# Building x * v of the next batch inside the last transform step of the current one

## The chip, the cores and the metric

The kernel runs on one core of a Trainium2 chip. The metric is the device time of one execution in microseconds (us), the median of several runs. A ratio is the mean time of one kernel's fast runs over the mean of the other's fast runs of the same rounds, so it isn't quite the ratio of the medians.

Names: PE is the matmul engine (PEld its weight loads), DVE the vector engine, ACT the scalar engine, POOL the GpSimd engine, SP the engine that issues the DMAs.

## The reference

Two blocks follow each other. The first is a long causal convolution over 12,480 positions for 4 batches of 128 channels, the second an MLP over the 49,920 rows of its result.

```python
# x, v: (4, 12480, 128); w_in: (128, 2048); w_out: (2048, 128), all float32
u = x * v
y = irfft(rfft(u, n=2*S) * rfft(h_filt, n=2*S))[:, :S]   # along the sequence
z = (x * y).reshape(B * S, D)
h = z @ w_in
out = (h * np.cos(h)) @ w_out
```

## The kernel before

The convolution is done by matmuls in five stages for each batch: x\*v ("u"), first transform ("f1"), second transform with the product by the filter ("f2"), first inverse ("i1"), last inverse with the product by x ("i2"). All stages work in one large SBUF tile, `slots`. The MLP (called MoE here, as in the code) runs over tiles of 480 rows, in 16 steps a tile. Batch 0 is convolved alone; the convolutions of batches 1 to 3 run between the MoE steps of the rows that are ready.

One MoE step:

```python
ph = ps_h.tile(...)                                   # 4 PSUM buffers
nc.tensor.matmul(ph, w_in_sb[:, c * P:(c + 1) * P], ats[n], ...)
nc.scalar.activation(a, ph, AF.Identity, bias=quarter, scale=INV_TWO_PI)
nc.vector.tensor_scalar(out=k, in0=a, scalar1=ROUND, scalar2=ROUND, ...)  # DVE
nc.gpsimd.tensor_tensor(f, a, k, op=ALU.subtract)                         # POOL
nc.scalar.activation(cs, f, AF.Sin, scale=TWO_PI)     # one step later
nc.vector.tensor_tensor(gt, ph, cs, op=ALU.mult)      # DVE, frees ph
nc.tensor.matmul(acc, w_out_sb[:, c, :], gt, ...)     # four steps later
```

The u stage, a group of 4 rows at a time, two of them mirrored about the middle (cut):

```python
def after(j, _):
    for half in range(2):
        engine.tensor_tensor(xt[:, half, :], xt[:, half, :], vt[:, half, :], op=ALU.mult)
        yield
    # both sums of the mirrored halves, written into slots
    for place, op, e in ((a, ALU.add, nc.gpsimd), (ODD + a, ALU.subtract, nc.vector)):
        e.tensor_tensor(u[0:R, :, place:place + UA, :]..., below, above, op=op)
    yield
```

The order of a convolution, with the share of it that each MoE step carries (cut):

```python
def conv_units(bank, b):
    yield from u_units(b, 4, slots[0:R, :, :, :], nc.vector)
    for i, steps in enumerate(f1_units(bank, slots[0:R, :, :, :])): ...
    yield from f2_units(bank, f2_product)
    for i, steps in enumerate(i1_units(bank)): ...
    yield from i2_units(bank, b)      # tm and xs: 3 buffers, asked for 2 groups ahead

U_STEPS, F1_STEPS, F2_STEPS, I1_STEPS, I2_STEPS = 2.75, 0.8, 2.9, 0.8, 1.6
```

The `*_STEPS` say how many MoE steps one unit of a stage is to lie beside. `tm` is a table of 312 KB a group that i2 multiplies with; it comes from DRAM each time.

## Time and profile before

The kernel took 4146.25 us in the median of the 3 runs known before the change (4143.87 to 4154.5). The profile's lines for its stages, and how to read them, are in the prediction below. What a stage costs **beyond** its MoE steps, at the 1.66 us that a step takes alone, is the measure used throughout: it adds up over the whole program, whereas busy shares don't.

The account further down counts a step where its first activation begins; the prediction counts another instruction (k), and the two differ by one here and there. So the stages u, f1, f2, i1 and i2 of batch 1 stand at 36.9, 45.2, 48.4, 56.0 and 53.8 us here, and f1, f2 and i1 at 43.5, 50.2 and 54.4 in the prediction. Batches 2 and 3 are the same within 4 us a stage.

### The profile page before, as it was taken

To read this page: it belongs to the slowest core of one execution; us is meant where nothing else is said; L and a number is where in the kernel's file an instruction comes from. 1 tells how busy PE (TensorE), PEld (TensorE's weight loads), DVE (VectorE), ACT (ScalarE), POOL (GpSimd) and SP (SyncE) were. 2 spreads that over 40 slices of the span, in tenths; PEclk is the share of its full clock that TensorE was granted. 3 is DMA by queue.
4 is the path that set the end of the run, shared out by engine and by line. 5 is a ranking of instruction groups with operands and counts; after the bars stand their busy time and mean duration, and the time that the engine had idled before them with its cause. 6 is when DMAs were issued, how large, how long until landed. Compare 5 with 4: busy or idle time off the path is not lost.

```text
span 4148.7 us, 49336 instructions
## 1 busy us (share of the span) xinstructions
PE 3885.9 (94%) x13882; PEld 2254.5 (54%) x13882; DVE 3050.5 (74%) x6420; ACT 2534.8 (61%) x4692; POOL 2614.4 (63%) x2441
## 2 busy tenths in 40 slices
PE   5958788899999998999999999999999999999999
PEld 3836583465556653555556644655566544444444
DVE  8657678997888569878876599778765566666666
ACT  1344055686667555666665466766664677777777
POOL 2521556777886457558864477488744577777776
PEclk7567799999999999999999999999999999999999
DMA  3253433212221443112211532022105300000000
GB/s 88 80 162 114 127 109 102 71 53 70 80 71 49 138 143 87 31 40 78 80 30 54 181 95 64 26 66 80 57 15 149 92 20 20 19 20 15 19 20 15
DMA packets 271766, 293.66 MB, mean 71 GB/s; under 512 B 16741, under 2 KB 204101, under 8 KB 271237
## 3 DMA queue, kind: packets, MB, share of 16 engines
q1 hardware_dynamic: 271493, 290.50, 24.0%
q8 instruction: 112, 1.84, 0.2%
q14 instruction: 161, 1.32, 0.1%
HBM read 210.12 MB, written 80.31 MB: 70 GB/s over the span
## 4 chain that ended last, share of the span: by engine, by line
PE 70%; POOL 10%; DVE 7%; DMA 5%; ACT 4%; issue 3%; SPq 0%; POOLq 0%; DVEq 0%; ACTq 0%
PE ph L598 25%; PE acc L622 20%; POOL f L607 7%; PE cv L622 5%; PE cv L415 4%; PE cv L396 4%; PE ps L350 3%; PE cv L365 2%; PE cv L350 2%; ACT cs L612 2%; DMA w<-wd 2%; DVE k L604 2%; PE ph L116 2%; POOL slots L344 1%; DMA hd<-h 1%
## 5 line engine op out<-in xcount | busy, mean ns | idle before, releaser
L607 POOL TENSOR_TENSOR f<-a,k 128x480 f32<-128x480 f32 x1664 | 2003.2, 1204 | 1096.1 <-DVE k L604 1075.1
L598 PE MATMUL ph<-at,w_in_sb 128*128 128x480 f32 x3328 | 1639.9, 574 | 43.7 <-DVE gt L614 41.9
L601 ACT ACTIVATE a<-ph,quarter 128x480 f32<-128x480 f32 x1664 | 1095.2, 658 | 665.1 <-PE ph L598 620.5
L622 PE MATMUL acc<-gt,w_out_sb 128*128 128x480 f32 x2784 | 1364.7, 572 | 16.7 <-ACT ot L627 16.2
L614 DVE TENSOR_TENSOR gt<-ph,cs 128x480 f32<-128x480 f32 x1664 | 1092.0, 656 | 310.9 <-ACT cs L612 283.2
L612 ACT ACTIVATE cs<-f 128x480 f32<-128x480 f32 x1664 | 999.2, 600 | 506.4 <-POOL f L607 504.2
L604 DVE TENSOR_SCALAR k<-a 128x480 f32<-128x480 f32 x1664 | 783.5, 471 | 569.4 <-ACT a L601 553.5
L622 PEld LDWEIGHTS acc<-gt,w_out_sb 128*128 128x128 f32 x2784 | 527.8, 191 | 631.3 <-issue 577.1
L598 PEld LDWEIGHTS ph<-at,w_in_sb 128*128 128x128 f32 x3328 | 592.5, 191 | 450.2 <-issue 271.7
L378 POOL TENSOR_TENSOR slots<-slots,t 120x256 f32<-120x256 f32 x384 | 306.0, 803 | 139.0 <-DVE t L377 132.9
L622 PE MATMUL cv<-gt,w_out_sb 128*128 128x480 f32 x544 | 263.2, 566 | 0.5 <-DVE gt L614 0.5
L365 PE MATMUL ps<-slots,w 124*120 124x256 f32 x384 | 164.5, 572 | 84.3 <-DVE w L250 48.7
L396 PEld LDWEIGHTS cv<-cs,slots 120*96 120x96 f32 x1536 | 178.2, 168 | 70.9 <-issue 58.4
L415 PEld LDWEIGHTS cv<-slots,tm 96*104 96x104 f32 x1440 | 175.4, 168 | 62.4 <-issue 51.5
L396 PE MATMUL cv<-cs,slots 120*96 120x120 f32 x1536 | 185.8, 267 | 7.2 <-POOL slots L378 7.2
L338 DVE TENSOR_TENSOR xt<-xt,vt 104x256 f32<-104x256 f32 x180 | 189.7, 1064 | 0.0
L415 PE MATMUL cv<-slots,tm 96*104 96x128 f32 x1440 | 183.5, 272 | 5.3 <-DMA tm<-td 5.3
L365 PE MATMUL cv<-slots,w 124*120 124x256 f32 x576 | 173.7, 382 | 7.0 <-DMA w<-wd 6.1
L365 PEld LDWEIGHTS ps<-slots,w 124*120 124x120 f32 x384 | 92.6, 267 | 156.2 <-issue 67.7
L350 PEld LDWEIGHTS cv<-c,slots 104*124 104x124 f32 x768 | 133.5, 194 | 66.3 <-issue 53.6
L365 PEld LDWEIGHTS cv<-slots,w 124*120 124x120 f32 x576 | 103.4, 184 | 117.6 <-issue 104.4
L622 PEld LDWEIGHTS cv<-gt,w_out_sb 128*128 128x128 f32 x544 | 103.2, 190 | 116.7 <-issue 114.5
(115 smaller groups left out, 3082.3 us busy)
## 6 DMA issues: line engine op xcount, KB each, us to landing
h<-hd SPq DMA_DIRECT2D x192, 240.0 KB
tm<-td SPq DMA_DIRECT2D x90, 312.0 KB
xt<-in_x_dram SPq DMA_DIRECT2D x120, 208.0 KB
vt<-in_v_dram SPq DMA_DIRECT2D x120, 208.0 KB
xs<-in_x_dram SPq DMA_DIRECT2D x120, 208.0 KB
zd<-zs SPq DMA_DIRECT2D x120, 208.0 KB
zb<-zd SPq DMA_DIRECT2D x104, 240.0 KB
out_dram<-ob SPq DMA_DIRECT2D x104, 240.0 KB
```

Source lines behind the costliest of these rows:

```text
L350: nc.tensor.matmul(ps[0:KE, i * 2 * N1:(i + 1) * 2 * N1], u[:, b, 0:KE, i], c1[0:u.shape[0], :, :].rearrange("p r k -> p (r k)"), start=Tr ...
L365: nc.tensor.matmul(ps[0:N2, i * 2 * D:(i + 1) * 2 * D], w[:, i, :], parts[0:KE, :, k1 + i, :, :], start=True, stop=True)
L378: nc.gpsimd.tensor_tensor(y[:, r], y[:, r], t[:, r], op=op)
L396: nc.tensor.matmul(ps[0:N1, (i * 2 + r) * N2:(i * 2 + r + 1) * N2], parts[0:N2, r, :, b, i], cs[:, r:r + 2, :].rearrange("p c a -> p (c a) ...
L415: nc.tensor.matmul(ps[0:R, i * D:(i + 1) * D], t[:, i, r, :], slots[0:N1, :, place, :], start=(r == 0), stop=(r == 1))
L598: nc.tensor.matmul(ph[:, 0:TOK], w_in_sb[:, c * P:(c + 1) * P], ats[n][:, :], start=True, stop=True)
L601: nc.scalar.activation(a[:, :], ph[:, 0:TOK], AF.Identity, bias=quarter[:, 0:1], scale=INV_TWO_PI)
L604: nc.vector.tensor_scalar(out=k[:, :], in0=a[:, :], scalar1=ROUND, scalar2=ROUND, op0=ALU.add, op1=ALU.subtract)
L607: nc.gpsimd.tensor_tensor(f[:, :], a[:, :], k[:, :], op=ALU.subtract)
L612: nc.scalar.activation(cs[:, :], f[:, :], AF.Sin, scale=TWO_PI)
L614: nc.vector.tensor_tensor(gt[:, :], ph[:, 0:TOK], cs[:, :], op=ALU.mult)
L622: nc.tensor.matmul(accs[n][:, 0:TOK], w_out_sb[:, c, :], gt[:, :], start=(c == 0), stop=(c == NFC - 1))
```

## The change

Its intent is to put the DVE work of u beside the PE work of i2. While i2 of batch b reads `slots`, u of batch b+1 writes into the places just read. For that, i2 must go through mirrored pairs of rows as u does, so each group stores z in two pieces. i2 is stretched to 3.4 MoE steps a group where it holds u. To make room in SBUF, `tm` and `xs` get two buffers there instead of three. Batch 1's u stays a stage of its own, and the whole of batch 1 is squeezed into 368 MoE steps, because its convolution has to be ready in time and now includes u of batch 2.

The core of the diff (cut: the helper for the mirrored order, the split store of z, and the same reordering in the table builder):

```diff
-    U_STEPS, F1_STEPS, F2_STEPS, I1_STEPS, I2_STEPS = 2.75, 0.8, 2.9, 0.8, 1.6
+    U_STEPS, F1_STEPS, F2_STEPS, I1_STEPS, I2_STEPS = 2.2, 0.9, 3.1, 0.9, 1.6
+    I2U_STEPS = 3.4
...
+    def n2s(g):
+        a = g * UA
+        return [*range(H - UA - a, H - a), *range(H + a, H + UA + a)]
...
     def conv_units(bank, b):
-        yield from u_units(b, 4, slots[0:R, :, :, :], nc.vector)
...
-        yield from i2_units(bank, b)
+        if b + 1 == B:
+            yield from i2_units(bank, b, 3)
+            return
+        new = u_units(b + 1, 3, slots[0:R, :, :, :], nc.vector, side="right")
+        for i, steps in enumerate(i2_units(bank, b, 2)):
+            if i >= 4:
+                for _ in range(1 + i % 2):
+                    next(new, None)
+            yield steps * I2U_STEPS / I2_STEPS
+        for steps in new:
+            yield steps
...
+            here = NT * NFC - 3 * NFC
+            less = here / (CONV_STEPS + H // UA * U_STEPS)
+            for steps in u_units(1, 4, slots[0:R, :, :, :], nc.vector):
+                yield steps * less
```

More of the change, by code (lines that the diff above doesn't have):

```diff
@@ L318, in filter_out, with load_group @@
                             below, above, op=op)
+    def n2s(g):
+        a = g * UA
+        return [*range(H - UA - a, H - a), *range(H + a, H + UA + a)]
+    def load_group(t, src, b, a):
+        first = src[b, H - UA - a:H - a, :]
+        nc.sync.dma_start(t[:, :, :], bass.AP(
+            tensor=first.tensor, offset=first.offset,
+            ap=[[N2 * D, R], [(UA + 2 * a) * D, 2], [1, UA * D]]))
     def clear_gap(u):
@@ L328, in u_load @@
             t = pool.tile([R, 2, UA * D], F32, name=name, bufs=n)
-            first = src[b, H - UA - a:H - a, :]
-            nc.sync.dma_start(t[:, :, :], bass.AP(
-                tensor=first.tensor, offset=first.offset,
-                ap=[[N2 * D, R], [(UA + 2 * a) * D, 2], [1, UA * D]]))
+            load_group(t, src, b, a)
             tiles.append(t)
@@ L411, in i2_mm @@
         for i in range(part * G // 2, (part + 1) * G // 2):
-            n2 = g * G + i
+            n2 = n2s(g)[i]
             places = (n2 - H, 2 * H + n2) if n2 >= H else (N2 - 1 - n2, N2 + H - 1 - n2)
@@ L416, in i2_mm @@
                                  slots[0:N1, :, place, :], start=(r == 0), stop=(r == 1))
-    def block(src, b, n2):
-        return src[b, :, :].rearrange("(p n) d -> p n d", n=N2)[:, n2, :]
     def i2_out(pool, ps, xs, b, g):
-        zs = pool.tile([R, G, D], F32, name="zs")
+        zs = pool.tile([R, 2, UA, D], F32, name="zs")
         nc.vector.tensor_tensor(
-            zs[:, :, :], ps[0:R, :].rearrange("p (g d) -> p g d", g=G), xs[:, :, :],
-            op=ALU.mult)
-        nc.sync.dma_start(zd[b, :, g * G:(g + 1) * G, :], zs[:, :, :])
+            zs[:, :, :, :].rearrange("p h n d -> p (h n d)"), ps[0:R, :],
+            xs[:, :, :].rearrange("p h n -> p (h n)"), op=ALU.mult)
+        for h in range(2):
+            n2 = n2s(g)[h * UA]
+            nc.sync.dma_start(zd[b, :, n2:n2 + UA, :], zs[:, h, :, :])
         yield
@@ L454 @@
     REST = 1.5
-    U_STEPS, F1_STEPS, F2_STEPS, I1_STEPS, I2_STEPS = 2.75, 0.8, 2.9, 0.8, 1.6
-    CONV_STEPS = (H // UA * U_STEPS + CB * (F1_STEPS + I1_STEPS) + N1 // 2 * F2_STEPS
-                  + N2 // G * I2_STEPS + 5 * REST)
+    U_STEPS, F1_STEPS, F2_STEPS, I1_STEPS, I2_STEPS = 2.2, 0.9, 3.1, 0.9, 1.6
+    I2U_STEPS = 3.4
+    CONV_STEPS = (CB * (F1_STEPS + I1_STEPS) + N1 // 2 * F2_STEPS + N2 // G * I2U_STEPS
+                  + 4 * U_STEPS + 5 * REST)
     def u_units(b, bufs, u, engine, side="left"):
@@ L523, in i1_units, with i2_units @@
                              lambda j, ps: i1_evict(pool, ps, j), 2)
-    def i2_units(bank, b, make=None):
+    def i2_units(bank, b, bufs, make=None):
         with tc.tile_pool(name="back", bufs=2) as pool:
@@ L529, in before @@
             def before(j):
-                ts[j] = pool.tile([N1, G, 2, R], F32, name="tm", bufs=3)
+                ts[j] = pool.tile([N1, G, 2, R], F32, name="tm", bufs=bufs)
                 if make is None:
@@ L534, in before @@
                     for i in range(G):
-                        make(ts[j][:, i, :, :], j * G + i)
-                xss[j] = pool.tile([R, G, D], F32, name="xs", bufs=3)
-                nc.sync.dma_start(xss[j][:, :, :],
-                                  block(x, b, slice(j * G, (j + 1) * G)))
+                        make(ts[j][:, i, :, :], n2s(j)[i])
+                xss[j] = pool.tile([R, 2, UA * D], F32, name="xs", bufs=bufs)
+                load_group(xss[j], x, b, j * UA)
             def mm(j, ps, i):
@@ L546, in i2_units @@
             yield from units(N2 // G, I2_STEPS, before, mm,
-                             lambda j, ps: i2_out(pool, ps, xss.pop(j), b, j), 2)
+                             lambda j, ps: i2_out(pool, ps, xss.pop(j), b, j), 2,
+                             ahead=bufs - 1)
     def t_units():
@@ L554, in t_units @@
                 for i in range(G):
-                    make_third(pool, t[:, i, :, :], g * G + i)
+                    make_third(pool, t[:, i, :, :], n2s(g)[i])
                     yield
@@ L720 @@
             with tc.tile_pool(name="spare", bufs=2) as pool:
-                for _ in i2_units(bank, 0, lambda t, n2: make_third(pool, t, n2, bank)):
+                for _ in i2_units(bank, 0, 3, lambda t, n2: make_third(pool, t, n2, bank)):
                     pass
@@ L737, in convolutions @@
             nonlocal ready
+            here = NT * NFC - 3 * NFC
+            less = here / (CONV_STEPS + H // UA * U_STEPS)
+            for steps in u_units(1, 4, slots[0:R, :, :, :], nc.vector):
+                yield steps * less
             for b in range(1, B):
-                yield from conv_units(bank, b)
+                for steps in conv_units(bank, b):
+                    yield steps * (less if b == 1 else 1.0)
                 ready = b
         conv = convolutions()
-        share = CONV_STEPS / (NT * NFC - 2 * NFC - 4)
         owed = 0.0
@@ L775 @@
                     moe_store(mpool, n - 1, ots.pop(n - 1))
-            owed += share
+            owed += 1.0
             while owed > 0.0:
```

## The prediction

> **What bounds the kernel now.** I read the page's slices first, then the trace cut into stages, then single instructions. The kernel has three regimes: the first batch's convolution alone (0 to 640 us), three more convolutions run between the steps of the MoE loop (640 to 3265 us), and the MoE loop alone. In the slices of the page (busy tenths, 40 equal slices of the span):
>
> ```profile
> PE   5958788899999998999999999999999999999999
> DVE  8657678997888569878876599778765566666666
> POOL 2521556777886457558864477488744577777776
> ```
>
> PE is at nine tenths nearly everywhere from the seventh slice on; after that DVE reaches nine in three places only, once in each convolution. The next view gives the busy time by engine in five stages of one convolution (batch 1) and in the MoE loop alone. The columns are the stretch, its length, then busy us and instruction counts of PE, weight loads, DVE, ACT, POOL, then the granted clock, DMA share and GB/s. The stages are, in order: x*v ("u"), first transform, second transform, first inverse, last inverse ("i2"), then MoE alone.
>
> ```profile
> 645.00:816.40 171.40, 151.50 (x360) 63.21 (x360) 164.68 (x253) 100.99 (x177) 131.05 (x112) 0.97 0.28 79
> 816.40:944.60 128.20, 127.27 (x482) 81.80 (x482) 120.05 (x266) 109.46 (x236) 91.80 (x91) 1.00 0.18 50
> 954.30:1231.90 277.60, 276.55 (x809) 146.61 (x810) 223.87 (x459) 179.74 (x299) 237.29 (x229) 0.99 0.27 78
> 1239.40:1380.10 140.70, 140.28 (x745) 94.54 (x746) 114.04 (x265) 100.04 (x231) 90.97 (x91) 0.99 0.15 43
> 1384.90:1516.70 131.80, 131.79 (x693) 90.50 (x694) 67.56 (x123) 58.60 (x103) 55.91 (x48) 1.00 0.59 175
> 3300.00:4100.00 800.00, 800.00 (x2164) 388.03 (x2163) 525.22 (x963) 632.75 (x1052) 579.44 (x481) 1.00 0.07 19
> ```
>
> The reader is to see two things. In u, DVE is busy 164.7 of 171.4 us (96%) and PE is not: PE has no work of the convolution there. In i2 it is the reverse: PE 100%, DVE 51%, POOL 42%. So u is bound by DVE, all else by PE.
>
> Counting one instruction of each MoE step (L604) in the same stretches gives 81, 51, 137, 52, 47 and 482 steps. Alone, a step costs 800/482 = 1.66 us. What a stage costs **beyond its MoE steps** is then: u 171.4 - 81*1.66 = 36.9 us; first transform 43.5; second 50.2; first inverse 54.4; i2 131.8 - 47*1.66 = 53.8. The last four are mostly PE's own work (i2 alone has 480 matmuls); the 36.9 of u is PE waiting. The chain inside u is shown by its waits:
>
> ```profile
> ACT cs L612 <- POOL f L607: 64.0, 77, 1.2
> PEld ph L598 <- DVE gt L614: 45.1, 48, 2.1
> POOL f L607 <- DVE k L604: 40.5, 53, 1.7
> ```
>
> PE waits for the gate product on DVE, to get a PSUM buffer back. The instructions that fill DVE there are the product x*v and the sums:
>
> ```profile
> L338 DVE TENSOR_TENSOR xt<-xt,vt x180: 409/974/1393, 645.0 to 2572.3; 104x256 f32<-104x256 f32 x180
> ...
> L344 DVE TENSOR_TENSOR slots<-xt x90: 425/924/1078, 648.8 to 2572.7; 104x256 f32<-104x256 f32 x90
> ```
>
> After the colon stand the shortest, median and longest duration in ns: 409 against 974 for one and the same shape.
>
> **What the Trainium skill says.** (1) "Perfetto Trace Analysis", Identifying the Most-Contended Engine: matmul busy is no measure of nearness to the limit, since matmuls are pipelined. I therefore use elapsed us per MoE step, not PE's 94%. The trace agrees that busy misleads: a step alone takes 1.66 us, though its four matmuls are listed with about 570 ns each, 2.28 us. (2) "SBUF — State Buffer", Who interferes with whom: a DVE instruction with two SBUF inputs contends with a GpSimd instruction that reads SBUF, by an exclusive lock. The trace agrees: the product takes 409 ns at the least and 974 in the median, and the POOL subtraction beside it takes 1204. So half of u's DVE time is waiting for POOL. (3) "PSUM — Partial Sum Buffer", Engine vs sequencer instructions: VectorE's queue is strict FIFO. So a product blocked by POOL also holds back the MoE's next k; the 40.5 us that POOL waited for k above fit that. (4) "DMA: Bandwidth & Descriptors", Specifications: transfers of 512 B or more reach line rate. The trace agrees: a 1,024 B packet in u took 56.8 ns and a 2,048 B one in i2 110.5 ns, 18.0 and 18.5 B/ns. So reading x and writing z in 1 KB pieces instead of 2 KB costs little.
>
> **The change, part by part.** I built the changed kernel, without running it, and read MoE steps per stage off its instruction order. Convolution 1 now gets u 54, then 47, 121, 47 and i2 83; convolutions 2 and 3 get 57, 147, 57 and i2 101 (with the next u inside) and 47 (last, nothing inside). Convolutions end at MoE step 1061 instead of 1138. MoE work is unchanged, so only the time beyond 1.66 us a step matters.
>
> - Removed: the u stages of batches 2 and 3: 2 * 36.9 = **-73.8 us** of PE waiting.
> - u of batch 1 stays, and is squeezed into 54 steps. DVE there: k and gt are 32.6/81 + 0.656 = 1.06 us a step, 57 us; products and sums were (63.9 + 28.3)/90 = 1.02 us, 92 us: 149 us. But two u operations now often stand side by side in the order, and the second of a pair doesn't wait behind a fresh f, so I take 0.8 to 1.02 us: 129 to 149, say 139. Beyond MoE 139 - 54*1.66 = 49, against 36.9: **+12** (5 to 20).
> - i2 with u inside, batch 1: PE needs 83*1.66 + 53.8 = 191.6 us. DVE needs 83*1.06 + 30*0.68 (the output product) + 85 u operations: 195 us at 1.02, 176 at 0.8. Near a tie: **+8** (0 to 15). For batch 2: PE 101*1.66 + 53.8 = 221.5, DVE 214 or 195: **+3** (0 to 8). The order puts one product right after the output product, which covers most of f's 1.2 us, so the shorter figure is the likelier.
> - About five u yields remain after each such i2, with the last group's three operations in a burst (8*0.96 = 8 us of DVE against some 8 MoE steps): **+6** for both.
> - Other stages: batch 1's are tighter by a tenth (**+3**), those of batches 2 and 3 looser, with more steps to hide DVE and POOL work behind (**-5**).
> - Convolutions end 77 steps, some 5 tiles, earlier; from then on every second tile's accumulator has a bank of its own. PE's weight loads waited 50.2 us in 43 waits for the eviction, 1.2 each; about half saved on 5: **-3**.
> - Batch 0's i2 stores z in two DMAs per group; DVE waited 19 us on those stores there: **+2**.
> - DMA: i2 moved 175 GB/s at 0.59 of the engines; now per group (312 + 4*208 KB) in 6.4 to 7.4 us, 155 to 179 GB/s: about the same share. Buffers of tm and xs fall from 3 to 2, but a group lasts 1.5 times as long: 0.
>
> Sum: -73.8 + 12 + 8 + 3 + 6 + 3 - 5 - 3 + 2 = -48. 4146 - 48 = **4098 us** (-1.2%).
>
> **Rivals.** (a) DVE becomes the bound of i2: every u operation keeps its 1.02 us and delays pile up in the strict FIFO. For it: DVE would be at 97 to 102% of PE's need. Against: the pairing above, and four PSUM buffers for the up product. It would add some 20 to 30 us: 4118 to 4128. (b) A DMA wait replaces the DVE one: with two buffers, tm of the next group starts only after the group before the present one was read, behind u loads that hold the one in-order SP queue for a product. For it: tm is 312 KB, and two buffers leave one group ahead. Against: about 8 us from issue to need by the order, and only 5.3 us of PE idle before L415 for tm in all of the kernel before. If 2 us were lost in each of 60 groups: 4218 at the worst. (c) PE simply takes all: no cost in i2 or after it, u of batch 1 no worse: 4146 - 74 - 8 = 4064, the floor. (d) The compressed batch 1 loses as much as batches 2 and 3 gain, by waits in all its stages: about 4146. Against: its other stages had DVE and POOL at 81 to 94% or lower.
>
> **Range and chances.** The likely misses are +30 (a, part of b) and -30 (c), with 3 us of noise: 4068 to 4135. Faster by 2% means below 4063, under the floor of (c): 0.06. Slower by 2% needs (b) at its worst: 0.02. Within 2%: 0.92.
>
> **What would show it right or wrong.** Right: i2 of batches 1 and 2 takes 192 to 207 and 222 to 230 us, with PE near 100% and DVE 85 to 95%; u of batch 1 takes 129 to 149 us with DVE over 95%; the products' median inside i2 falls below 974 ns; no u stage between i2 and the first transform; the MoE loop alone still 1.66 us a step. Wrong: PE waiting on tm's DMA in i2 by over 20 us (b), DVE at 97% there and PE waiting for gt (a), or first and second transforms of batch 1 costing over 10 us more beyond their steps (d).

## The result

The changed kernel takes **4094.12 us** (4 runs, 4092.5 to 4094.84) against 4149.16 us (4 runs) of the kernel before on the same chip. The ratio is 0.9867, with a 95% interval of 0.985 to 0.9884: faster by 1.3%, clear of noise. (e9_depth34 below, the same kernel with one more buffer, was correct.)

The slices of the page of the changed kernel, to be held against those of before:

```profile
PE   5957787899999999999999999999999999999999
DVE  8657677998887877788668877877656666666666
POOL 1521545778875665788546657885446777777776
```

DVE reaches nine only once now, in u of batch 1 and the stage behind it. The other two peaks are gone.

The view by stretches of the changed kernel has the columns named in the prediction (PE, PEld, DVE, ACT, POOL, clock, DMA share, GB/s). In order: u of batch 1, i2 of batch 1 with u of batch 2 inside, i2 of batch 2 with u of batch 3 inside, the last i2 with nothing inside, and MoE alone.

```profile
646.90:776.70 129.80, 102.64 (x232) 41.37 (x232) 127.69 (x200) 66.60 (x117) 96.06 (x84) 0.95 0.34 97
...
1296.30:1491.40 195.10, 195.10 (x853) 120.54 (x854) 154.34 (x274) 105.37 (x181) 123.86 (x110) 0.98 0.65 186
...
2110.70:2333.80 223.10, 223.09 (x933) 134.16 (x934) 172.44 (x310) 129.43 (x220) 145.06 (x128) 0.99 0.57 165
2947.30:3080.90 133.60, 133.55 (x693) 91.35 (x694) 67.81 (x123) 58.64 (x103) 56.67 (x47) 0.99 0.60 171
3200.00:4000.00 800.00, 800.00 (x2165) 388.13 (x2164) 525.84 (x962) 633.27 (x1052) 580.03 (x482) 1.00 0.07 19
```

In both stages that hold u, PE is busy all the time, and DVE 79% and 77% of it (154.34 of 195.10, 172.44 of 223.10). u of batch 1 remains as it was, only shorter, since it holds fewer MoE steps: DVE 98%, PE 79%.

One line of the source, the product x\*v, asked for three times: in u of batch 1, in i2 of batch 1 and in i2 of batch 2. After the colon stand the shortest, median and longest duration in ns.

```profile
L346 DVE TENSOR_TENSOR xt<-xt,vt x60: 409/1010/1546, 646.9 to 774.9; 104x256 f32<-104x256 f32 x60
```

```profile
L346 DVE TENSOR_TENSOR xt<-xt,vt x54: 415/643/1082, 1321.9 to 1491.9; 104x256 f32<-104x256 f32 x54
```

```profile
L346 DVE TENSOR_TENSOR xt<-xt,vt x53: 415/484/1081, 2138.0 to 2331.1; 104x256 f32<-104x256 f32 x53
```

The same instruction takes 1010 ns in the median in the separate stage and 643 and 484 ns inside i2. The shortest ones, 409 to 415 ns, are taken as its own work and the rest as waiting; e2_psum below bears this out.

The whole account, from the traces (before 4148.7 us, after 4093.0 us), in us beyond 1.66 us a step:

| part | before | after | difference | predicted |
|---|---|---|---|---|
| u of batches 2 and 3 | 74.0 | - | -74.0 | -73.8 |
| u of batch 1 | 36.9 | 41.9 | +5.0 | +12 |
| i2 of batch 1, with u inside | 53.8 | 57.3 | +3.5 | +8 |
| i2 of batch 2, with u inside | 53.8 | 55.4 | +1.6 | +3 |
| from i2 to the next stage, batches 1 and 2 | -0.5 | 8.8 | +9.3 | +6 |
| f1, f2, i1 of batch 1 and the gaps between | 160.1 | 154.2 | -5.9 | +3 |
| the same of batches 2 and 3 | 304.9 | 304.6 | -0.3 | -5 |
| i2 of batch 3 | 53.8 | 55.5 | +1.7 | 0 |
| MoE alone at the end | 11.0 | 11.1 | +0.1 | -3 |
| batch 0, up to the start of u | 638.3 | 641.9 | +3.6 | +2 |
| sum | | | -55.4 | -48 |

The traces differ by 55.7 us; the rest is rounding. (u starts 1.9 us later, at 646.9 and not at 645.0 us, but with 3 MoE steps begun before it instead of 4.) Each row comes from one trace: i2 of batch 0 alone took 69.4 to 73.6 us in six runs that have the same code for it, so a row of 2 to 4 us is not clear of noise.

### The profile page after: what moved, and what is told of

The parts are those of the page before. It is cut to its first block, busy times and chain, and to the rows that moved or that the text cites. A ratio compares the mean times of both kernels' runs of the same rounds, so it can differ in the third digit from the quotient of the medians.

```text
span 4093.0 us, 49612 instructions
## 1 busy us (share of the span) xinstructions
PE 3850.8 (94%) x13882; PEld 2256.8 (55%) x13882; DVE 2990.2 (73%) x6420; ACT 2548.1 (62%) x4692; POOL 2605.6 (64%) x2441
## 4 chain that ended last, share of the span: by engine, by line
PE 78%; DVE 6%; POOL 5%; DMA 5%; ACT 3%; issue 2%; SPq 0%; DVEq 0%; POOLq 0%; ACTq 0%
PE ph L618 29%; PE acc L642 23%; PE cv L642 6%; PE cv L423 4%; PE cv L404 4%; POOL f L627 3%; PE ps L358 3%; PE cv L373 3%; PE cv L358 2%; PE ph L116 2%; DMA w<-wd 2%; DMA hd<-h 2%; PE ps L404 1%; ACT cs L632 1%; POOL slots L386 1%
## 5 line engine op out<-in xcount | busy, mean ns | idle before, releaser
L642 PE MATMUL acc<-gt,w_out_sb 128*128 128x480 f32 x2720 | 1327.0, 570 | 9.5 <-ACT ot L647 8.9
L624 DVE TENSOR_SCALAR k<-a 128x480 f32<-128x480 f32 x1664 | 798.2, 480 | 537.7 <-ACT a L621 519.9
L642 PEld LDWEIGHTS acc<-gt,w_out_sb 128*128 128x128 f32 x2720 | 515.0, 190 | 603.7 <-issue 566.5
L642 PE MATMUL cv<-gt,w_out_sb 128*128 128x480 f32 x608 | 294.1, 566 | 0.5 <-DVE gt L634 0.5
L642 PEld LDWEIGHTS cv<-gt,w_out_sb 128*128 128x128 f32 x608 | 115.4, 190 | 130.3 <-issue 128.3
L358 PE MATMUL cv<-c,slots 104*124 104x192 f32 x768 | 155.1, 329 | 10.4 <-POOL slots L352 8.9
```

The costliest lines, as they stand in the source:

```text
L358: nc.tensor.matmul(ps[0:KE, i * 2 * N1:(i + 1) * 2 * N1], u[:, b, 0:KE, i], c1[0:u.shape[0], :, :].rearrange("p r k -> p (r k)"), start=Tr ...
L624: nc.vector.tensor_scalar(out=k[:, :], in0=a[:, :], scalar1=ROUND, scalar2=ROUND, op0=ALU.add, op1=ALU.subtract)
L642: nc.tensor.matmul(accs[n][:, 0:TOK], w_out_sb[:, c, :], gt[:, :], start=(c == 0), stop=(c == NFC - 1))
```

## The experiments

Ten kernels were run, each beside the kernel before on the same chip. The medians of before were 4150.34 us for the first four runs, 4154.14 us for the next four and 4154.05 us for the last two. I compare ratios to it; 0.9867 is the changed kernel.

| run | what | us | ratio to before |
|---|---|---|---|
| - | the change | 4094.12 | 0.9867 |
| e1_serial | all of the change but the overlap | 4159.12 | 1.0024 |
| e2_psum | product in u of batch 1 reads PSUM (wrong result) | 4075.40 | 0.9820 |
| e3_i2pace | i2 with u at 1.6 steps a group | 4150.53 | 1.0001 |
| e4_burst | x\*v of a group as one burst on DVE | 4084.37 | 0.9845 |
| e5_noload | e3 without the loads of x and v (wrong result) | 4108.76 | 0.9890 |
| e6_depth | e3 with three buffers for tm | 4109.32 | 0.9888 |
| e7_spread | e4's instructions, one in a turn | 4083.90 | 0.9832 |
| e8_first | e4, and batch 1's u begun in batch 0's i2 | 4073.14 | 0.9801 |
| e9_depth34 | the change with three buffers for tm | 4095.36 | 0.9860 |
| e11_best | e8 with three buffers for tm | 4076.36 | 0.9807 |

### Is it the overlap?

e1_serial keeps the mirrored order, the split stores and the squeezed batch 1. It undoes the overlap, and with it what came for its sake: i2 goes at 1.6 steps a group and with three buffers again.

```diff
-        new = u_units(b + 1, 3, slots[0:R, :, :, :], nc.vector, side="right")
-        for i, steps in enumerate(i2_units(bank, b, 2)):
-            ...
+        yield from i2_units(bank, b, 3)
+        yield from u_units(b + 1, 4, slots[0:R, :, :, :], nc.vector)
```

Expected:

> The changed kernel with its mirrored order, its split stores and its pacing, but x*v of the next batch run after the last inverse instead of inside it. Theory (the gain is the two separate DVE-bound x*v stages, and nothing else of the change): two x*v stages of about 66 MoE steps and 145 to 152 us come back, each about 38 us beyond 66*1.66 us; total 4150 to 4175 us, as slow as the kernel before or slower, since batch 1 stays squeezed. Rival (pacing, the mirrored order or the earlier end of the convolutions carry part of the gain): total 4100 to 4135 us.

Measured: 4159.12 us, ratio 1.0024 (1.0009 to 1.0039). The two u stages that came back, in the view by stretches:

```profile
1426.20:1553.10 126.90, 100.60 (x233) 41.20 (x231) 125.09 (x195) 65.19 (x115) 93.53 (x82) 0.94 0.37 109
...
2290.80:2434.80 144.00, 122.64 (x290) 50.74 (x288) 139.99 (x218) 80.67 (x141) 108.35 (x94) 0.96 0.33 97
```

DVE is busy 99% and 97% of them and PE 79% and 85%. They hold 51 and 64 MoE steps, so they cost 42.2 and 37.8 us beyond their steps. Everything but the overlap is worth nothing here; it even costs 0.24%, as a squeezed batch 1 should. The overlap, with the stretched pace that goes with it, is worth 1.0024 - 0.9867 = 1.6% of the time before. Both stages were shorter than the 145 to 152 us I expected, the first by far (126.9 us, for 51 steps and not 66), since its batch is squeezed too.

### What fills DVE in u?

e2_psum takes away what makes the product wait, in u of batch 1 alone: its second operand comes from a PSUM bank of ones instead of the SBUF tile of v. The result is wrong. v is still loaded.

```diff
-        engine.tensor_tensor(xt[:, half, :], xt[:, half, :], vt[:, half, :], op=ALU.mult)
+        engine.tensor_tensor(xt[:, half, :], xt[:, half, :],
+                             vt[:, half, :] if other is None else other, op=ALU.mult)
```

> Wrong result on purpose: in the x*v stage of batch 1 alone the product reads its second operand from a PSUM bank of ones instead of the SBUF tile of v (v is still loaded). Theory (what fills DVE there is waiting for POOL's subtraction, because of two SBUF inputs): the product's median falls from 1010 ns to about 410 to 450 ns, that stage from 130 us to 97 to 108 us, the total to 4062 to 4076 us. Rival (the product's duration is its own work, or the stage hangs on POOL or on loads): the stage stays above 122 us and the total above 4085 us.

Measured: 4075.4 us, ratio 0.9820. The groups of instructions in u of batch 1, changed kernel first, then e2_psum (busy us, mean ns, idle time before and its releaser):

```profile
L346 DVE TENSOR_TENSOR xt<-xt,vt 104x256 f32<-104x256 f32 x60 | 59.8, 1011 | 0.0
...
L624 DVE TENSOR_SCALAR k<-a 128x480 f32<-128x480 f32 x54 | 22.1, 409 | 0.6 <-ACT a L621 0.6
```

```profile
L630 DVE TENSOR_SCALAR k<-a 128x480 f32<-128x480 f32 x54 | 33.3, 617 | 3.3 <-ACT a L627 3.1
...
L346 DVE TENSOR_TENSOR xt<-xt,cv 104x256 f32<-104x256 f32 x60 | 23.6, 410 | 0.0
```

The product falls from 1011 to 410 ns, by 36 us for 60 of them. But k, the MoE's own instruction, grows from 409 to 617 ns, by 11 us for 54. The stage falls by 17.5 us, from 129.8 to 112.3 us, and the whole trace by 18.1 us, from 4093.0 to 4074.9. So the theory holds: most of the product's duration was waiting, and the stage hangs on it. It was too simple in one point, and the stage missed the 97 to 108 us I expected. The wait is partly handed on to k, which comes after it in DVE's queue. And DVE is no longer full: it idles for 13 of 112.4 us (2 of 129.8 before), 9.1 of them with gt waiting for cs, so DVE alone no longer bounds the stage.

### What would have been lost without the stretched pace?

e3_i2pace sets `I2U_STEPS` back to 1.6.

```diff
-    I2U_STEPS = 3.4
+    I2U_STEPS = 1.6
```

> The changed kernel with 1.6 instead of 3.4 MoE steps for each group of the last inverse, as before the change, with x*v still inside it (44 and 47 steps instead of 83 and 101). Theory A (DVE has little slack there, so the stretched stage is needed): PE need 47*1.66 + 53.8 = 132 us, DVE 50 + 20 + 85 operations at 0.53 to 0.9 us = 115 to 147 us; the stages take 140 to 155 us, with PE waiting for gt; total 4105 to 4125 us. Theory B (inside this stage the products hardly wait for POOL, so PE stays the bound at any pace): the stages take 127 to 137 us, total 4088 to 4100 us.

Measured: 4150.53 us, ratio 1.0001 (0.9986 to 1.0016). **All of the gain is gone.** Both theories missed: the stages are longer than either allowed, and the cause is neither's. i2 of batches 1 and 2:

```profile
1359.20:1518.70 159.50, 138.23 (x677) 92.50 (x678) 108.00 (x196) 54.56 (x96) 76.71 (x71) 0.95 0.76 218
2131.90:2294.90 163.00, 141.83 (x693) 93.64 (x694) 112.83 (x203) 58.80 (x103) 80.82 (x74) 0.96 0.74 215
```

They cost 86.4 and 84.9 us beyond their steps, against 57.3 and 55.4. Yet DVE is busy only 68% and 69%, and no engine is full. DVE as the bound (theory A) can't be the reason. The last two columns point elsewhere: the DMA engines are busy 76% and 74%, with 218 and 215 GB/s. And so does one wait, here of the first and then of the second stage:

```profile
PE cv L423 <- DMA tm<-td: 24.3, 16, 4.0
...
PE cv L423 <- DMA tm<-td: 19.8, 14, 3.5
```

PE waited 16 and 14 times for tm, 24.3 and 19.8 us in all. From the trace I took, for each group but a stage's first, the time from SP's issue of tm to its last packet, and from there to the first matmul that uses it. Before the change tm took 3.3 us in the median and was there 6.5 us ahead. In the changed kernel it was there 2.8 us ahead in i2 of batch 1 and 4.8 us ahead in that of batch 2; the least were 0.5 and 1.9 us. At 1.6 steps a group it took 4.5 to 4.7 us and came 0.9 to 1.0 us before its use; with 30 waits of PE for it, that is just in time and often late. So I formed a new theory: with one group of look-ahead, the landing of tm bounds i2 when a group gets short. Two runs test it at the pace of e3.

e5_noload leaves the loads of x and v out after the first groups (wrong result), with all other work the same. e6_depth keeps them, and gives tm a third buffer and two groups of look-ahead; the SBUF it needs was just there.

```diff
 # e5_noload, in u_load
+            if once is not None and (name, a // UA % n) in once:
+                tiles.append(once[name, a // UA % n])
+                continue
```

```diff
 # e6_depth, in i2_units; xs stays one group ahead
-                ts[j] = pool.tile([N1, G, 2, R], F32, name="tm", bufs=bufs)
+                ts[j] = pool.tile([N1, G, 2, R], F32, name="tm", bufs=3)
...
-                             ahead=bufs - 1)
+                             ahead=2)
```

> Wrong result on purpose: the run with 1.6 MoE steps for each group of the last inverse (stages of 159 and 163 us there against 127 and 132 us that PE needs, DVE busy 69%), but x and v of batches 2 and 3 are loaded for the first groups only and the same tiles are used again, so DVE, POOL and PE do the same work and 2 * 208 KB a group are not moved. Theory (transfers bound that stage: the third-tile tm lands 0.9 us before its use there, in the median, with 215 GB/s moved): stages 128 to 142 us, total 4085 to 4106 us. Rival (products in the FIFO of DVE bound it): stages 152 us or more, total 4136 us or more.

> The run with 1.6 MoE steps for each group again, all loads kept, but tm has three buffers and is asked for two groups ahead instead of one. Theory L (what bounds the stage is the time from asking to landing, about 4.4 us, with one group ahead): stages 128 to 145 us, total 4085 to 4115 us. Theory B (the rate of the transfers bounds it: 1144 KB a group at 215 GB/s are 5.3 us): stages 153 us or more, total 4138 us or more.

Measured: 4108.76 and 4109.32 us, ratios 0.9890 and 0.9888. The same two stages, e5_noload first:

```profile
1359.90:1498.50 138.60, 133.42 (x677) 91.75 (x678) 108.22 (x196) 54.62 (x96) 76.54 (x71) 0.95 0.59 171
2112.40:2254.20 141.80, 137.22 (x693) 93.20 (x694) 112.24 (x203) 58.77 (x103) 80.96 (x74) 0.96 0.60 169
```

```profile
1366.00:1505.20 139.20, 133.43 (x677) 90.48 (x678) 105.21 (x196) 56.29 (x96) 79.42 (x70) 0.97 0.86 246
2119.00:2258.20 139.20, 135.33 (x693) 91.49 (x694) 108.89 (x201) 60.19 (x102) 84.17 (x73) 0.99 0.88 248
```

Either cure takes 20 to 24 us out of each stage. e6 moves the same bytes faster, at 246 and 248 GB/s, so 215 GB/s was not the limit of the transfers; asking earlier was enough. e5's total is 3 us above the range I had set for it. PE's waits for tm show directly in the traces: they fall from 24.3 and 19.8 us to 5.6 and 6.7 in e5 and to 9.6 and 5.2 in e6, so 13 to 19 us of the 20 to 24 are tm coming late. What the cures took beyond that isn't separated; both also change when the other loads go out. At the short pace each stage stood 31 to 33 us above i2's own 53.8, and 7 to 12 us of this stay in both runs. tm is still nearly late in both, 1.6 to 1.7 us ahead in e5 and 1.2 to 1.3 in e6, where it now takes 5.4 to 5.6 us from issue to last packet, the DMA engines are 86 to 88% busy and DVE waits for v. I have not separated it further.

e9_depth34 asks whether the changed kernel itself, at 3.4, still loses to this. It has e6's edit and nothing else.

> The changed kernel at its own pace (3.4 MoE steps a group), with the one difference that tm has three buffers and is asked for two groups ahead. Theory (at this pace tm lands 2.8 and 4.8 us before its use in the median, so one group ahead hides it): stages 192 to 196 and 221 to 224 us, total within 6 us of the changed kernel's 4094 us. Rival (some groups still wait for tm, and the pace was won by luck of the mean): 4074 to 4087 us.

Measured: 4095.36 us, ratio 0.9860 (0.9841 to 0.9879): the same as the change. tm now comes 9.3 and 12.0 us ahead in the median, and the two stages take 193.1 and 223.0 us instead of 195.1 and 223.1. At 3.4 steps one group of look-ahead does hide tm. At most 2 us of batch 1's stage are due to it.

### Can u of batch 1 be made shorter?

It is the one u stage left, bound by DVE. In u of batches 1 to 3, e4_burst makes one product of 104x512 of the two, moves the sum that POOL made to DVE, and issues all three in a row. e7_spread issues the same three instructions, each in its own turn.

```diff
 # e4_burst, in u_units.after
+                    yield
+                    nc.vector.tensor_tensor(xt[:, :, :], xt[:, :, :], vt[:, :, :], op=ALU.mult)
+                    u_sums(u, tiles.pop(j), j * UA, nc.vector)   # both sums on DVE
+                    yield
```

```diff
 # e7_spread
+                    nc.vector.tensor_tensor(xt[:, :, :], xt[:, :, :], vt[:, :, :], op=ALU.mult)
+                    yield
+                    for one in u_sums(u, tiles.pop(j), j * UA, nc.vector):
+                        yield
```

> The changed kernel with the x*v work of a group of batches 1 to 3 as one burst on DVE: one product of 104x512 instead of two of 104x256, and both sums on DVE instead of one on POOL. Theory (each separate DVE operation with two SBUF inputs waits once for a subtraction that POOL has begun; a burst waits once): x*v of batch 1 falls from 130 us to 105 to 120 us, the last inverse stays within 3 us; total 4070 to 4086 us. Rival (the sum of work counts, and DVE has now a sum more, or a burst of 2 us holds up the gate product): stage 130 us or more, total 4094 us or more.

> The same x*v instructions as in the burst run (one product of 104x512, both sums on DVE), but each in its own turn, with MoE instructions between. Theory (each separate operation with two SBUF inputs waits for a subtraction begun on POOL): the sums' median rises from 0.42 to over 0.7 us, x*v of batch 1 takes 122 to 132 us, total 4082 to 4096 us. Rival (the gain of the burst run is the sum taken from POOL and the instruction saved): x*v of batch 1 takes 112 to 122 us, total 4068 to 4084 us.

Measured: 4084.37 and 4083.90 us, ratios 0.9845 and 0.9832. Both are ahead of the change, e4 by so little that its interval (0.9829 to 0.9862) still touches the change's, and they equal each other within the noise: u of batch 1 takes 122.9 and 123.0 us instead of 129.8. The groups in that stage, e4_burst first:

```profile
L631 DVE TENSOR_SCALAR k<-a 128x480 f32<-128x480 f32 x53 | 34.9, 659 | 1.2 <-ACT a L628 1.2
...
L352 DVE TENSOR_TENSOR slots<-xt 104x256 f32<-104x256 f32 x60 | 22.9, 423 | 1.0
```

```profile
L352 DVE TENSOR_TENSOR slots<-xt 104x256 f32<-104x256 f32 x60 | 46.1, 785 | 0.4
...
L633 DVE TENSOR_SCALAR k<-a 128x480 f32<-128x480 f32 x54 | 21.5, 399 | 1.1 <-ACT a L630 1.0
```

In the burst the sums don't wait (423 ns) and k does (659). Spread, the sums wait (785) and k doesn't (399). The order only decides which instruction waits, and the stage takes as long. So my theory that a burst saves the waits falls, though e7's numbers taken alone came in as it said and only e4's stage missed (105 to 120 us expected): had a burst saved waits, e4's stage would be the shorter. What e4 and e7 share, one instruction less a group in all and POOL freed of a sum, is what is left to explain the gain; neither was tested apart.

### Combining what was learned

e8_first puts over half of batch 1's u (16 of 30 groups) into i2 of batch 0, on top of e4. e11_best adds tm's third buffer.

```diff
-                for _ in i2_units(bank, 0, 3, lambda t, n2: make_third(pool, t, n2, bank)):
-                    pass
+                for i, _ in enumerate(i2_units(
+                        bank, 0, 3, lambda t, n2: make_third(pool, t, n2, bank))):
+                    if i >= 4:
+                        next(u1, None)      # u1 = u_units(1, 3, slots..., nc.vector, side="right")
```

> A candidate for the best version: the burst run, with the larger part of batch 1's x*v (some 19 of 30 groups) put into the last inverse of batch 0, where no MoE step runs yet. Theory (PE stands still for 16% of that stage and DVE for 37%, and outside it a group costs over a microsecond of idle PE): that stage grows from 71 to 85 to 105 us, what is left of the separate x*v stage takes 42 to 52 us, total 4058 to 4082 us. Rival (DVE and POOL are as full there as anywhere): total 4084 us or more.

> The best version so far (x*v of batch 1 begun in batch 0's last inverse, bursts on DVE; 4073 us on another chip or day) with three buffers for tm. Theory: the stages of the last inverse with x*v inside are at PE's bound already (beyond 1.66 us a step 56.6 and 56.5 us against 53.8), so at most 5 us: 4066 to 4076 us. Rival: 4060 us or less.

Measured: 4073.14 us (0.9801, interval 0.9787 to 0.9816) and 4076.36 us (0.9807). i2 of batch 0 and u of batch 1, in the changed kernel and then in e8_first:

```profile
556.80:630.40 73.60, 60.99 (x480) 57.24 (x480) 46.49 (x107) 44.15 (x118) 55.88 (x80) 0.95 0.57 165
646.90:776.80 129.90, 102.67 (x233) 41.40 (x233) 127.79 (x200) 66.60 (x117) 96.17 (x84) 0.95 0.33 97
```

```profile
555.10:643.00 87.90, 70.26 (x480) 67.80 (x480) 70.92 (x155) 44.25 (x118) 64.02 (x81) 0.81 0.73 221
643.00:711.50 68.50, 45.87 (x100) 18.49 (x100) 50.26 (x89) 30.02 (x51) 26.84 (x22) 0.85 0.37 106
```

i2 of batch 0 grows by 14 us, within what I expected. Much of that is PE itself: its 480 matmuls take 70.3 us instead of 61.0, at a granted clock of 0.81 instead of 0.95 (67.8 us at 0.84 in e11_best). Why the clock is lower there no run shows. The rest of u looks longer than my 42 to 52 us, but its stretch here includes the gap behind i2, which is 16.5 us in the changed kernel. So I count from the start of i2 to f1: the changed kernel takes 220.0 us with 56 MoE steps, 127.0 us beyond them; e8_first takes 156.4 us with 24 steps, 116.6 beyond. e8_first is the fastest version, 0.66% under the change on ratios, and correct. tm's third buffer adds nothing to it (the total is 0.4 us above the range I gave): PE is already busy all the time in the stages it would help. A version with all of batch 1's u in batch 0's i2 deadlocked, so whether more is to be had there stays open.

## Why the prediction was right

The time, 4098 us against 4094.12, was right well inside its range, and the mechanism was the one forecast. By its own steps:

- **The bound.** u bound by DVE, with PE waiting, and the other stages by PE: shown by e1_serial (the stages come back, and the time with them) and e2_psum (a wait taken from DVE shortens the stage by 17.5 us and the kernel by 18.1). One reading was too strong. What products and sums took there beyond their shortest durations is 63.9 - 60*0.409 + 28.3 - 30*0.425 = 54.9 us: a third of the stage's 164.7 us of DVE, not half.
- **Removed, -73.8.** The account gives -74.0.
- **u of batch 1, +12 (5 to 20).** It was +5.0; with the prediction's own count of steps, 54, it was +3.3 and below the range. The term that was mis-sized is DVE's time, 139 us. The u operations took 59.8 us for 60 products and 22.8 for 30 sums, 0.92 us each, within my 0.8 to 1.02. But I had added durations as if DVE's instructions never overlapped. With k (22.1) and gt (35.8) they sum to 140.5 us, in a stage of 129.8 where DVE was busy 127.7. This was to be seen before the change: 63.9 + 28.3 + 32.6 + 53.8 = 178.6 us, in a stage of 171.4. The timeline of DVE in that stage before the change (start, duration, instruction) shows how:

```profile
700.14 0.66 DVE L614 TENSOR_TENSOR gt<-ph,cs 128x480 f32<-128x480 f32 x1
700.72 0.93 DVE L344 TENSOR_TENSOR slots<-xt 104x256 f32<-104x256 f32 x1
701.57 0.40 DVE L604 TENSOR_SCALAR k<-a 128x480 f32<-128x480 f32 x1
```

The second and the third begin 0.08 us before their predecessor's end (700.14 + 0.66 = 700.80 against 700.72). In u of batch 1 after the change 164 such overlaps, of 0.06 to 0.09 us, make up the 13 us.
- **i2 with u inside, +8 and +3.** They were +3.5 and +1.6. I had DVE 85 to 95% busy there and it was 79 and 77%, since all u operations, products and sums, took 0.59 and 0.54 us in the mean and not 0.8. The reason I gave, that the output product covers POOL's subtraction, fits the products' lower medians; but k's mean rose there to 548 ns in batch 2, so some of the wait had moved again, as in e2_psum. No run tests that reason.
- **Leftover of u behind i2, +6.** It was +9.3.
- **Other stages, +3 for batch 1 and -5 for the others.** They were -5.9 and -0.3, so the signs of both were wrong, with little effect on the sum. Most of batch 1's gain is a single gap between f1 and f2, 6.5 us beyond before and 1.0 after. Before the change PE stood there for a table of f2:

```profile
PE cv L365 <- DMA w<-wd: 6.1, 1, 6.1
```

SP had waited 9.5 us for ACT to finish a tile that an output store needed, and the load of w came after that store (issued at 950.15 and 950.55 us, f1 having ended at 944.6). In the changed kernel no such store stands before it, nor in e1_serial, where the gap is 2.8 us as well. So 5.5 us of the gain come from where the new pacing happens to put a store. That was not forecast, and it is luck.
- **Accumulator, -3.** At the end, where I had put it, nothing is seen (+0.1).
- **DMA, 0.** Right within 2 us for this kernel (e9_depth34), but for a narrower reason than I gave. I said about 8 us from issue to need and no loss. (The 155 to 179 GB/s took a KB as 1000 bytes; with 1024 they are 158 to 183, and 165 and 186 were measured, the MoE's transfers included.) The margin left by the time of use was 2.8 us in the median of batch 1's stage, and e3_i2pace shows what lies right behind it.
- **Rivals.** (a), DVE as the bound of i2, did not happen, and not even at 1.6 steps, where DVE was 69% busy. (b), a wait for tm in place of the one on DVE, was the real danger: not in the change, but at the old pace the whole gain was gone, and either cure brought 1.1 of its 1.3% back. (c), the floor of 4064, was missed by 30 us. (d) did not happen.

So the mechanism was right, and the large term with it. The smaller terms were not: several were too large, some had the wrong sign, and they partly cancelled. That the total came within 4 us is in part luck.

## What to carry to other kernels

Price a stage by its time beyond what the bounding engine needs for the work that runs beside it, not by busy shares; those numbers add up, and this prediction stood on them. Work that blocks one engine is best put where another engine is the bound, but check what the move takes from the buffers: a tile that was asked for two groups ahead and is now asked for one group ahead may be hidden only as long as a group is long. When two engines hold each other up, changing the order of instructions can move the wait without shortening the stage; taking an instruction away, or moving it to where the engine has slack, did shorten it here.

## What the Trainium skill lacked or had wrong

- "SBUF — State Buffer", Who interferes with whom: it says that one side blocks the other fully, and the runs agree (409 against 1010 ns for the product). It lacks that the wait moves on to the next DVE instruction that is subject to it. In e2_psum the product lost 601 ns and k gained 208; between e4_burst and e7_spread the sums went from 423 to 785 ns and k from 659 to 399, at 122.9 and 123.0 us for the stage.
- "Perfetto Trace Analysis", DVE / Act Engine Instruction: it says that the reported window runs up to the acknowledged write. Its section Optimizing Scalar/DVE Operations adds that the acknowledgement overlaps with the next instruction, and the trace agrees. It lacks what follows for sums of durations: in u before the change 173 overlaps of 0.07 to 0.09 us make the four groups of DVE sum to 178.6 us while DVE is busy 164.7.
- "DMA: Bandwidth & Descriptors", Latency and other measured facts: it names about 2 us as the fixed cost of a DMA. I found no page that says what a transfer of some hundred KB takes to land while the same queue carries much else. Here 312 KB took 3.3 us in the median from issue to last packet in i2 before the change, and 4.5 to 4.7 us in i2 of e3_i2pace at 215 to 218 GB/s.
- "Perfetto Trace Analysis", Identifying the Most-Contended Engine: it recommends MFU and the busy share of weight loads to judge PE. It lacks that the latter can't be compared between stages with different matmuls: it is 49% in MoE alone (388.0 of 800 us) and 69% in i2 before the change (90.5 of 131.8), with PE busy all the time in both. MFU was not worked out here.
